# An attention and MLP kernel on one core: a written order for the first head pairs, and float64 weights decoded with an integer addition

## The chip, the cores and the metric

The kernel runs on one core of a Trainium2 chip. The core has TensorE (PE, matrix products), VectorE (DVE), ScalarE (ACT), GpSimd (POOL) and SyncE (SP, which here issues most DMA transfers); each runs its own queue in order, and semaphores tie them together. SBUF is the memory on the chip with 128 partitions (rows), PSUM holds PE's results in banks. The metric is the device time of one execution in microseconds (us); a smaller time is better.

## The reference

Float32 attention with a local band and a few global keys, four batches of eight heads over 768 positions of 64 values, is followed by a gated MLP whose weights come as float64:

```python
scores = scale * np.matmul(q, k.transpose(0, 1, 3, 2))
keep = (pos[None, :] < n_global) | ((rel >= 0) & (rel < n_local))      # 8 and 96
scores = np.where(keep, scores - slopes * dist, -1e9)
a = exp(scores - max);  a = a / (sum(a) + 1e-9);  x = a @ v            # x: 3072 x 512
h = x @ w_in                                                           # 512 -> 2048
g = h * np.clip(h + 3.0, 0.0, 6.0) / 6.0
out = (g @ w_out).astype(np.float32)                                   # 2048 -> 512
```

## The kernel before

**Work.** The 3072 tokens are eight blocks of 384. A block's attention goes by head pairs (four a block), a pair by three tiles of 128 queries. A tile's scores are 128 x 232 for each of two heads (96 earlier positions, 8 global ones, 128 of its own; 128 x 128 for a sequence's first tile). `scores` (matmul, line 765) writes them to PSUM; DVE adds a scaled distance and takes the row's minimum (L776, `n<-sp` or `n<-acc`); ACT takes exponentials and row sums (L780); `sum_up` (L788, L789, DVE) and `normalize` (L798 on POOL, L796 on DVE for the very first pair) scale the rows; `turn` has PE transpose them (L806, L808) and ACT evict them as `pt` (L810); `values` (L850) multiplies with v, and ACT and DVE split the result into a high and a low part, `xh` and `xl` (L150, L151).

**MLP.** The hidden width is cut into 16 parts f. For a block and an f, `first` does 12 matmuls (L164, `hp`), the gate makes `g`, `gh`, `gl` (L175 on ACT, L176 on DVE, L184 on ACT or L182 on POOL, L189 on DVE), and `second` does 9 matmuls (L196). One block and one f together, 21 matmuls, are called a PE block below.

**Weights.** They lie in HBM as float64, in 32 chunks of 128 x 512 (two 32-bit words each), one of `w_in` and one of `w_out` for every f. `fetch` loads chunk i into one of two buffers `wst`; the decoding makes a float32 of each and splits it into a high and a low part for PE. Per chunk: ACT takes the magnitude of the high word (L362) and later the high part (L406); DVE does seven operations (L381 clamp, L394 shift, L400 sign, L409 exponent, L384 low word times exponent, L398 float addition, L391 low part). `decode` is a generator that is advanced in four steps a chunk; `work(pe, dve)` adds up what PE and DVE are given in the written program and advances it whenever DVE has been given less than PE. `LEAD` is put on DVE's account at the start, so it sets how late the decoding begins.

**Start.** `banded_setup` blanks the halves of the q columns that must be zero (DVE memsets, L281), loads the first pairs' keys and q (`load`, L295: three transfers a pair for the first twelve pairs), and `banded_masks` makes the distances d0 and d1 on DVE from the two bounds, which come by a DMA on ACT's queue. `distances` scales them for each head (L323 on ACT for the first, L325 on POOL for the others). The first twelve pairs have unsplit operands and are worked on first; from the ninth pair on, the first MLP blocks run between them.

**What sets the order.** The instructions of PE, SP and POOL keep the order of the written program (`in_order`). ACT's and DVE's order is set by a scheduler, which simulates the program and may put an instruction ahead of one that is written before it.

Of the kernel before, what the change touches and what calls it, by code (L numbers as in the profile page):

```python
# [9 lines left out]
F32 = mybir.dt.float32  # L10
# [9 lines left out]
P = 128  # L20
# [14 lines left out]
VW = 2 * NT * P  # L35
LOAD = KW + QW + VW
# [10 lines left out]
LEAD = 5.0  # L47
# [9 lines left out]
class Kernel:  # L57
# [189 lines left out]
    def banded_masks(self, pool):  # L247
# [18 lines left out]
        ts(out=glo, in0=glo, scalar1=ng, scalar2=FAR, op0=ALU.is_ge, op1=ALU.mult)  # L266
        for d, cols in ((d0, slice(CB, W)), (d1, slice(0, W))):
            ts(out=far[:, cols], in0=rel[:, cols], scalar1=nl, scalar2=FAR, op0=ALU.is_ge, op1=ALU.mult)
            tt(out=d, in0=rel[:, cols], in1=far[:, cols], op=ALU.max)
            if d is d0:  # L270
                ts(out=glo, in0=glo, scalar1=nl, scalar2=None, op0=ALU.max)
                tt(out=d[:, 0:NG], in0=d[:, 0:NG], in1=glo, op=ALU.min)
            else:
                nc.vector.tensor_copy(out=d[:, PREV:CB], in_=glo)

    def rooms(self, pool, n, start=0):

        room = [pool.tile([P, LOAD], F32, name=f"load{start + i}") for i in range(n)]
        for i, at in enumerate(room):
            for j in range(2):  # L280
                self.nc.vector.memset(at[(1 - j) * D:(2 - j) * D, KW + j * TB:KW + (j + 1) * TB], 0.0)  # L281
        return room
# [21 lines left out]
    def loaded(self, n):  # L304
# [3 lines left out]
        q = at[:, KW:KW + QW].rearrange("p (j t c) -> p j t c", j=2, t=NT)  # L308
        v = at[:, KW + QW:LOAD].rearrange("p (s t c) -> p s t c", s=2, t=NT)
        return at[:, 0:KW], q, v[:, 0], v[:, 1]  # L310
# [28 lines left out]
    def banded_setup(self):  # L339
# [4 lines left out]
        self.room = self.rooms(self.const, ROOMS)  # L344
        self.iv = self.const.tile([P, 4], I32, name="iv")
# [582 lines left out]
```

## Time and profile before

| | us |
|---|---|
| median of 3 runs | 675.11 (674.5 to 675.69) |
| the profiled execution | 674.97 |
| its span, first to last instruction | 673.1 |
| PE busy in the span | 655.3 (97%) |
| DVE busy | 438.3 (65%) |
| ACT busy | 283.0 (42%) |
| POOL busy | 192.9 (29%) |

The profile is of one execution. Its span leaves out 1.87 us before the first and behind the last instruction. A busy PE is one with a matmul in it, at whatever pace; idle time of an engine costs only where another waits for it.

### The profile page before, as it was taken

The numbers are of one execution on the slowest core, as the hardware profiler recorded it, in microseconds if no ns is written. First come the engines' busy times: TensorE is split into PE (matmuls) and PEld (weight loads), VectorE is DVE, ScalarE is ACT, GpSimd is POOL, SyncE is SP. The second block draws the span as 40 slices with busy tenths as digits, with TensorE's granted clock in tenths as the row PEclk, the third lists the DMA queues.
The fourth block names the chain that finished last, engine by engine and source line by source line (L and its number), as shares of the span: only waits on it lengthen the run. The fifth ranks groups of instructions, "written<-read, shape, count | busy, mean of one in ns | idle before, by whom it ended". The sixth has DMA issues, their size and how long they took to land.

```text
span 673.1 us, 11323 instructions
## 1 busy us (share of the span) xinstructions
PE 655.3 (97%) x3905; PEld 588.5 (87%) x3905; DVE 438.3 (65%) x1186; ACT 283.0 (42%) x744; POOL 192.9 (29%) x354
## 2 busy tenths in 40 slices
PE   5999999999999999999999999999999999999996
PEld 4788889999999889899989999899989999989995
DVE  7789999999975666457653676447762666422221
ACT  6998755544446333144333433143331443131111
POOL 2765500000000443234340343315431343302110
PEclk9999999999999999999999999999999999999999
DMA  8677533333303456624654367534555255510001
GB/s 259 164 226 242 162 121 102 118 108 112 95 31 133 131 135 181 157 94 131 167 139 119 101 172 193 144 94 126 139 159 140 80 151 141 139 48 1 1 1 52
DMA packets 62611, 84.33 MB, mean 125 GB/s; under 512 B 8784, under 2 KB 48720, under 8 KB 62544
## 3 DMA queue, kind: packets, MB, share of 16 engines
q1 hardware_dynamic: 62256, 83.25, 43.1%
q8 instruction: 33, 0.54, 0.3%
q14 instruction: 34, 0.28, 0.1%
q10 hardware_dynamic: 288, 0.26, 0.1%
HBM read 62.52 MB, written 20.97 MB: 124 GB/s over the span
## 4 chain that ended last, share of the span: by engine, by line
PE 87%; DMA 4%; ACT 4%; DVE 2%; POOL 2%; issue 1%; SPq 0%; POOLq 0%; ACTq 0%
PE hp L164 38%; PE acc L196 32%; DMA wst<-w 4%; PE xp L850 2%; PE sp L769 2%; PE tp L850 2%; PE sp L196 2%; PE tp L196 2%; PE xp L196 2%; PE tp L769 2%; ACT n L780 2%; POOL n L798 1%; PE acc L765 1%; ACT pt L810 1%; PE acc L850 1%
## 5 line engine op out<-in xcount | busy, mean ns | idle before, releaser
L175 ACT ACTIVATE g<-hp,small 128x384 f32<-128x384 f32 x127 | 73.9, 582 | 256.2 <-PE hp L164 221.2
L164 PE MATMUL hp<-xh,w1h 128*128 128x384 f32 x512 | 174.0, 340 | 0.0
L164 PE MATMUL hp<-xh,w1l 128*128 128x384 f32 x512 | 172.8, 337 | 0.0
L164 PE MATMUL hp<-xl,w1h 128*128 128x384 f32 x512 | 171.9, 336 | 0.0
L182 POOL TENSOR_SCALAR gh<-g 128x384 fp32r<-128x384 f32 x96 | 57.8, 602 | 294.8 <-DVE g L176 264.9
L196 PE MATMUL acc<-w2h,gl 128*128 128x512 f32 x336 | 132.9, 395 | 0.1
L196 PE MATMUL acc<-w2l,gh 128*128 128x512 f32 x336 | 132.8, 395 | 0.0
L196 PE MATMUL acc<-w2h,gh 128*128 128x512 f32 x336 | 132.1, 393 | 0.0
L798 POOL TENSOR_SCALAR n<-n,sums 128x232 f32<-128x232 f32 (+1 forms) x186 | 105.0, 581 | 52.3 <-DVE sums L789 38.7
L176 DVE SCALAR_TENSOR_TENSOR g<-g,hp 128x384 f32<-128x384 f32 x128 | 70.2, 548 | 76.4 <-ACT g L175 75.9
L780 ACT ACTIVATE n<-n,least 128x232 f32<-128x232 f32 (+1 forms) x192 | 89.5, 468 | 39.2 <-DVE least L776 38.5
L189 DVE TENSOR_TENSOR gl<-g,gh 128x384 fp32r<-128x384 f32 x128 | 73.1, 571 | 45.7 <-POOL gh L182 44.1
L164 PEld LDWEIGHTS hp<-xh,w1h 128*128 128x128 f32 x512 | 96.3, 188 | 5.5 <-issue 1.5
L164 PEld LDWEIGHTS hp<-xl,w1h 128*128 128x128 f32 x512 | 96.2, 188 | 3.8
L164 PEld LDWEIGHTS hp<-xh,w1l 128*128 128x128 f32 x512 | 96.0, 188 | 0.0
L196 PEld LDWEIGHTS acc<-w2l,gh 128*128 128x128 f32 x336 | 63.0, 188 | 13.3
L196 PEld LDWEIGHTS acc<-w2h,gl 128*128 128x128 f32 x336 | 63.2, 188 | 11.8 <-DVE gl L189 1.5
L196 PEld LDWEIGHTS acc<-w2h,gh 128*128 128x128 f32 x336 | 63.3, 188 | 10.6 <-POOL gh L182 0.3
L823 DVE STREAM_TRANSPOSE blocks<-n 128x256 f32<-128x256 f32 x112 | 43.5, 424 | 25.7 <-POOL n L798 25.1
L743 POOL TENSOR_SCALAR kx<-load 64x504 fp32r<-64x504 f32 (+1 forms) x40 | 23.1, 577 | 119.2 <-PE hp L164 117.6
L776 DVE CUSTOM_DVE_ANT_0 n<-sp,d 128x232 f32<-128x232 f32 (+1 forms) x70 | 23.7, 376 | 37.1 <-PE sp L769 36.8
L780 ACT ACTIVATION_READ_ACCUMULATOR n<-n,least 128x1 f32 x192 | 36.5, 190 | 0.0
(111 smaller groups left out, 764.9 us busy)
## 6 DMA issues: line engine op xcount, KB each, us to landing
wst<-w SPq DMA_DIRECT2D x32, 512.0 KB, 3.5
there<-blocks SPq DMA_DIRECT2D x52, 256.0 KB, 2.6
load<-pairs SPq DMA_DIRECT2D x20, 636.0 KB, 5.3
load<-pairs SPq DMA_DIRECT2D x32, 384.0 KB, 4.1
weights<-there SPq DMA_DIRECT2D x48, 192.0 KB, 3.8
out<-o SPq DMA_DIRECT2D x23, 256.0 KB, 2.1
weights<-there SPq DMA_DIRECT2D x32, 160.0 KB, 3.3
load<-pairs SPq DMA_DIRECT2D x12, 252.0 KB, 4.5
```

What stands on the lines that cost most here:

```text
L164: self.nc.tensor.matmul(hp, lhsT=self.w1(w, f)[:, kt, :], rhs=a[:, kt, :], start=(n == 0), stop=(n == 3 * NKT - 1))
L175: nc.scalar.activation(out=g, in_=hp, func=AF.Relu, bias=self.three, scale=1.0)
L176: nc.vector.scalar_tensor_tensor(out=g, in0=g, scalar=6.0, in1=hp, op0=ALU.min, op1=ALU.mult)
L182: self.nc.gpsimd.tensor_scalar(out=gh, in0=g, scalar1=1.0, scalar2=0.0, op0=ALU.mult, op1=ALU.add)
L189: self.nc.vector.tensor_tensor(out=gl, in0=g, in1=gh.bitcast(F32), op=ALU.subtract)
L196: self.nc.tensor.matmul(acc[tt], lhsT=a[:, tk], rhs=self.w2(w, f), start=(f == 0 and j == 0), stop=(f == NF - 1 and j == 2))
L769: nc.tensor.matmul(sp[:, j, lo:W], lhsT=q[:, t], rhs=part["kx"][:, c], start=(m == 0), stop=(m == 1))
L776: nc.vector.tensor_tensor_reduce(out=e[:, j, lo:W], in0=sp[:, j, lo:W], in1=d, op0=ALU.add, op1=ALU.min, scale=scale, scalar=3.0e38, accum ...
L780: nc.scalar.activation(out=e[:, j, lo:W], in_=e[:, j, lo:W], func=AF.Exp, bias=self.least[:, i:i + 1], scale=-1.0, accum_out=self.sums[:, ...
L798: nc.gpsimd.tensor_scalar(out=e[:, j, lo:W], in0=e[:, j, lo:W], scalar1=over, scalar2=0.0, op0=ALU.mult, op1=ALU.add)
L823: nc.vector.transpose(out=blocks[:, :, s].rearrange("p b j q -> p j b q"), in_=e[:, :, c:c + P].rearrange("p j (b q) -> p j b q", b=4))
L850: nc.tensor.matmul(xps[j * D:(j + 1) * D, t * P:(t + 1) * P], lhsT=vt[0:K, t, j * D:(j + 1) * D], rhs=self.part(t, j, c, K), start=(c == 0 ...
```

## The change

Five things are edited. The columns of a load are laid out anew, so that the first twelve pairs need two transfers of 64 rows instead of three, and the second of the very first goes on ACT's queue; the blanks are one range a half, written by DVE for the first room, by POOL for the other two. The masks are made with fewer operations on DVE and the small ones on POOL. Four matmuls on constants are put ahead of everything on PE (`wake`). ACT and DVE keep the written order, too, until the loop reaches pair number `HEAD` = 1, and `LEAD` goes from 5 to 13. The decoding takes the low word on POOL, as a multiple of the last place, and DVE adds it to the bits as integers; the exponent (L409) and the product (L384) go, and a chunk is fetched one chunk earlier.

```diff
-LEAD = 5.0
+HEAD = 1
+LEAD = 13.0
+WAKE = 4
...
-        ts(out=glo, in0=glo, scalar1=ng, scalar2=FAR, op0=ALU.is_ge, op1=ALU.mult)
-        for d, cols in ((d0, slice(CB, W)), (d1, slice(0, W))):
-            ts(out=far[:, cols], in0=rel[:, cols], scalar1=nl, scalar2=FAR, op0=ALU.is_ge, op1=ALU.mult)
-            tt(out=d, in0=rel[:, cols], in1=far[:, cols], op=ALU.max)
...
+        pool_ts(out=glo, in0=glo, scalar1=ng, scalar2=FAR, op0=ALU.is_ge, op1=ALU.mult)
+        pool_ts(out=glo, in0=glo, scalar1=nl, scalar2=0.0, op0=ALU.max, op1=ALU.add)
+        ts(out=far, in0=rel, scalar1=nl, scalar2=FAR, op0=ALU.is_ge, op1=ALU.mult)
+        tt(out=d0, in0=rel[:, CB:W], in1=far[:, CB:W], op=ALU.max)
+        tt(out=d0[:, 0:NG], in0=d0[:, 0:NG], in1=glo, op=ALU.min)
+        tt(out=d1[:, 0:PREV], in0=rel[:, 0:PREV], in1=far[:, 0:PREV], op=ALU.max)
+        tt(out=d1[:, CB:W], in0=rel[:, CB:W], in1=far[:, CB:W], op=ALU.max)
+        nc.gpsimd.tensor_copy(out=d1[:, PREV:CB], in_=glo)
...
+    def blank(self, room, engine):
+
+        engine.memset(room[D:P, KQ:KW + QW], 0.0)
+        engine.memset(room[0:D, 0:TB], 0.0)
...
-                parts = [(slice(0, KW), slice(None))] + [(slice(KW + j * TB, KW + (j + 1) * TB), slice(j * D, (j + 1) * D)) for j in range(2)]
+                parts = [(slice(TB, KW + QW), slice(0, D)), (slice(0, KQ), slice(D, P))]
             for columns, rows in parts:
-                self.nc.sync.dma_start(out=self.place(n)[rows, columns], in_=self.pairs[n, rows, columns])
+                engine = self.nc.scalar if n == 0 and rows == slice(D, P) else self.nc.sync
+                engine.dma_start(out=self.place(n)[rows, columns], in_=self.pairs[n, rows, columns])
...
+    def wake(self):
+
+        any_ = self.three.broadcast_to([P, P])
+        out = self.ps_x.tile([P, BANK], F32, name="xp")[:, 0:P]
+        for _ in range(WAKE):
+            self.nc.tensor.matmul(out, lhsT=any_, rhs=any_, start=True, stop=True)
...
     def magnitude(self, i):
+        words = self.raw[i].rearrange("p (c w) -> p c w", w=2)
         self.z[i] = self.zp.tile([P, DM], I32, name="wz")
...
+        self.e[i] = self.ep.tile([P, DM], I32, name="we")
+        self.nc.scalar.activation(out=self.z[i].bitcast(F32), in_=words[:, :, 1].bitcast(F32), func=AF.Abs)
+        self.nc.gpsimd.tensor_scalar(out=self.e[i], in0=words[:, :, 0].bitcast(U32), scalar1=2.0 ** -29, scalar2=0.0, op0=ALU.mult, op1=ALU.add)
...
-                stt(out=e, in0=words(i - 1)[:, :, 0].bitcast(U32), scalar=2.0 ** -52, in1=e, op0=ALU.mult, op1=ALU.mult)
-                if i + 1 < N:
-                    self.fetch(i + 1)
...
-                tt(out=e, in0=self.z.pop(i - 1).bitcast(F32), in1=e, op=ALU.add)
...
-                ts(out=self.e[i], in0=z, scalar1=-0x00800000, scalar2=None, op0=ALU.bitwise_and)
...
+                if i + 2 < N:
+                    self.fetch(i + 2)
+            yield 0.6 * a
+            if a:
+                tt(out=z, in0=z, in1=self.e.pop(i), op=ALU.add)
...
+            yield 0.69 * a
...
-        self.in_order(start)
+        self.in_order(start, here(), (mybir.EngineType.PE, mybir.EngineType.SP, mybir.EngineType.Pool))
+        self.in_order(begin, head, (mybir.EngineType.Activation, mybir.EngineType.DVE), True)
```

The program's order shows it at three places. SP first, at the start: `load` is a room for a pair's keys, q (first transfers) and values (128x768), `wst` a weight chunk, and a number behind a name tells the rooms apart. Before:

```order
L295 DMA load_72<-pairs 128x504
L295 DMA load_72<-pairs 64x384 x2
L295 DMA load_73<-pairs 128x504
L295 DMA load_73<-pairs 64x384 x2
L357 DMA wst<-w 128x1024
L295 DMA load_164<-pairs 128x504
L295 DMA load_164<-pairs 64x384 x2
L357 DMA wst<-w 128x1024
L295 DMA load_72<-pairs 128x768
L295 DMA load_73<-pairs 128x768
L295 DMA load_72<-pairs 128x504
```

And of the change:

```order
L300 DMA load_72<-pairs 64x888
L300 DMA load_73<-pairs 64x888 x2
L300 DMA load_165<-pairs 64x888 x2
L300 DMA load_72<-pairs 128x768
L371 DMA wst<-w 128x1024
L300 DMA load_73<-pairs 128x768
L371 DMA wst<-w 128x1024
L300 DMA load_72<-pairs 64x888 x2
```

The first chunk has moved behind the third pair's keys and the first pair's values, and the fourth pair's keys (`load_72` again) follow the second chunk with one transfer fewer.

ACT next, from its first scaled distance `p` to the third pair's exponentials (`n,sums<-n,least`, two a tile); `wz<-wst` is a chunk's magnitude. Before:

```order
L323 ACTIVATE p_177<-d_91 128x128 x2
L780 ACTIVATE n,sums<-n,least 128x128 x2
L323 ACTIVATE p_178<-d_92 128x232
L780 ACTIVATE n,sums<-n,least 128x232
L362 ACTIVATE wz<-wst 128x512
L780 ACTIVATE n,sums<-n,least 128x232 x3
L780 ACTIVATE n,sums<-n,least 128x128 x2
L780 ACTIVATE n,sums<-n,least 128x232 x2
L362 ACTIVATE wz<-wst 128x512
L810 COPY pt<-tp 128x2x128
```

And of the change:

```order
L328 ACTIVATE p_179<-d_87 128x128 x2
L328 ACTIVATE p_180<-d_88 128x232
L797 ACTIVATE n,sums<-n,least 128x128 x2
L797 ACTIVATE n,sums<-n,least 128x232 x4
L797 ACTIVATE n,sums<-n,least 128x128 x2
L797 ACTIVATE n,sums<-n,least 128x232 x4
L797 ACTIVATE n,sums<-n,least 128x128 x2
L827 COPY pt<-tp 128x2x128
```

The second distance stands ahead of the first exponentials, and no magnitude stands between the exponentials of the first three pairs; the two magnitudes come six rows later.

DVE last, in the decoding while two token blocks share the weights. `g` and `gl` are the gate, `ISA` is the new addition. Before:

```order
L176 SCALAR_TENSOR_TENSOR g<-g,hp 128x384
L381 TENSOR_SCALAR wz<-wz 128x512
L384 SCALAR_TENSOR_TENSOR we<-wst,we 128x512
L394 TENSOR_SCALAR wz<-wz 128x512
L189 TENSOR_TENSOR gl<-g,gh 128x384
L398 TENSOR_TENSOR we<-wz,we 128x512
L400 SCALAR_TENSOR_TENSOR wz<-wst,wz 128x512
L176 SCALAR_TENSOR_TENSOR g<-g,hp 128x384
L409 TENSOR_SCALAR we<-wz 128x512
L391 TENSOR_TENSOR w2l_1350<-we,w2h_1349 128x512
```

And of the change:

```order
L179 SCALAR_TENSOR_TENSOR g<-g,hp 128x384
L413 ISA wz<-wz,we 128x1024
L398 TENSOR_SCALAR wz<-wz 128x512
L192 TENSOR_TENSOR gl<-g,gh 128x384
L399 TENSOR_SCALAR wz<-wz 128x512
L404 TENSOR_TENSOR w1l_1336<-wz,w1h_1335 128x4x128
L407 SCALAR_TENSOR_TENSOR wz<-wst,wz 128x512
L179 SCALAR_TENSOR_TENSOR g<-g,hp 128x384
```

A whole chunk now lies between two gates, in five operations; before, five of a chunk's seven lay between two gates.

## Rows read from the trace of the kernel before

**Rows 1.** Busy time by stretch: stretch, length, engines' busy us, clock, DMA share, GB/s.

```profile
0.00:5.16 5.16, 0.94 (x3) 0.77 (x4) 3.44 (x14) 1.49 (x3) 1.41 (x10) 1.00 0.51 154
5.16:22.17 17.01, 13.08 (x79) 10.49 (x80) 13.92 (x71) 12.79 (x47) 7.72 (x17) 1.00 0.81 245
22.17:57.17 35.00, 33.47 (x287) 28.68 (x286) 30.89 (x130) 33.65 (x113) 21.74 (x42) 1.00 0.77 222
57.17:95.00 37.83, 36.63 (x272) 32.30 (x273) 35.83 (x90) 26.69 (x70) 14.82 (x22) 1.00 0.54 171
95.00:205.00 110.00, 110.00 (x551) 99.43 (x550) 100.11 (x202) 54.29 (x97) 1.22 (x2) 1.00 0.28 91
205.00:673.00 468.00, 461.22 (x2720) 416.84 (x2718) 254.10 (x686) 154.13 (x418) 145.95 (x263) 1.00 0.43 118
```

**Rows 2.** PE's waits in the first 22 us: total, times, longest.

```profile
PE sp L765 <- DMA load<-pairs: 4.2, 1, 4.2
```

**Rows 3.** PE's waits from 22 to 95 us.

```profile
PE tp L806 <- POOL n L798: 1.4, 4, 0.6
PE tp L806 <- ACT pt L810: 1.2, 3, 0.5
```

**Rows 4.** The chain that ended last: start, length in us, what.

```profile
4.22 5.97 DMA wst<-w
...
95.07 2.08 PE acc L196 x9
97.16 2.10 PE hp L164 x12
```

**Rows 5.** Timeline of ACT: start, length, what, idle time before it.

```profile
10.21 0.67 ACT L362 ACTIVATE wz<-wst 128x512 f32<-128x512 f32 x1 [1.78 <-DMA wst<-w]
```

**Rows 6.** Timeline of DVE in the first 8 us.

```profile
1.00 2.89 DVE L281 MEMSET load<- 64x384 f32 x6
3.89 0.17 DVE L263 CAST fv<-iv 128x4 f32<-128x4 int32 x1
...
7.41 0.40 DVE L776 CUSTOM_DVE_ANT_0 n<-acc,p 128x232 f32<-128x232 f32 x1
```

**Rows 7.** DMA issues of the first 8 us: KB each, us to landing.

```profile
load<-pairs SPq DMA_DIRECT2D x3, 252.0 KB, 3.3
load<-pairs SPq DMA_DIRECT2D x6, 96.0 KB, 3.5
iv<-bounds ACTq DMA_DIRECT2D x1, 2.0 KB, 3.1
```

**Rows 8.** Timeline of PE in the first 22 us.

```profile
5.48 3.06 PE L765 MATMUL acc<-load 128*128 128x232 f32 x8
...
8.82 1.73 PE L765 MATMUL acc<-load 128*128 128x232 f32 x8
...
20.73 1.32 PE L850 MATMUL xp<-pt,load 128*64 128x128 f32 x20
```

**Rows 9.** Groups of DVE from 95 to 205 us: busy us, mean ns, idle.

```profile
L176 DVE SCALAR_TENSOR_TENSOR g<-g,hp 128x384 f32<-128x384 f32 x27 | 14.9, 550 | 6.4 <-ACT g L175 6.3
L384 DVE SCALAR_TENSOR_TENSOR we<-wst,we 128x512 f32<-128x512 uint32 x21 | 14.3, 683 | 0.0
L398 DVE TENSOR_TENSOR we<-wz,we 128x512 f32<-128x512 f32 x21 | 14.3, 683 | 0.0
```

**Rows 10.** Timeline of DVE around 101 us.

```profile
101.33 0.68 DVE L398 TENSOR_TENSOR we<-wz,we 128x512 f32<-128x512 f32 x1
101.93 0.42 DVE L394 TENSOR_SCALAR wz<-wz 128x512 int32<-128x512 int32 x1
```

**Rows 11.** The page's costliest groups, one of POOL.

```profile
L182 POOL TENSOR_SCALAR gh<-g 128x384 fp32r<-128x384 f32 x96 | 57.8, 602 | 294.8 <-DVE g L176 264.9
```

**Rows 12.** Groups of DVE from 60 to 95 us.

```profile
L398 DVE TENSOR_TENSOR we<-wz,we 128x512 f32<-128x512 f32 x6 | 4.4, 736 | 0.0
```

**Rows 13.** Groups of POOL from 60 to 95 us.

```profile
L798 POOL TENSOR_SCALAR n<-n,sums 128x232 f32<-128x232 f32 x12 | 9.6, 815 | 0.0
```

More of the change, by code (lines that the diff above doesn't have):

```diff
@@ L458, in banded @@
     def banded(self, flag):
+        here = lambda: len(self.nc.cur_bb.bb.instructions)
+        begin = here()
         self.banded_setup()
-        start = len(self.nc.cur_bb.bb.instructions)
+        start = here()
         self.common(2, 2)
@@ L486, in banded @@
                 self.room += self.rooms(self.pool("more", 1, ctx=ctx), MORE - ROOMS, ROOMS)
+                self.blank(self.room[2], self.nc.gpsimd)
                 self.load(2, False)
+                self.load(0, True)
+                self.fetch(0)
+                self.load(1, True)
                 self.fetch(1)
[L489 to L490 removed]
                 self.plain_distances(ctx)
@@ L563, in banded, with in_order @@
         self.finish()
-        self.in_order(start)
+        self.in_order(start, here(), (mybir.EngineType.PE, mybir.EngineType.SP, mybir.EngineType.Pool))
+        self.in_order(begin, head, (mybir.EngineType.Activation, mybir.EngineType.DVE), True)
         return acc
-    def in_order(self, start):
+    def in_order(self, start, end, engines, first=False):
         last = {}
-        for i in self.nc.cur_bb.bb.instructions[start:]:
-            if i.engine in (mybir.EngineType.PE, mybir.EngineType.SP, mybir.EngineType.Pool) and "Tile" not in type(i).__name__:
+        for n, i in enumerate(self.nc.cur_bb.bb.instructions[start:None if first else end], start):
+            if i.engine in engines and "Tile" not in type(i).__name__:
                 if i.engine in last:
@@ L574, in in_order @@
                         mybir.DependencyClass.NoSync, mybir.DependencyReason.DATA), reason="in_order")
-                last[i.engine] = i.name
+                if n < end:
+                    last[i.engine] = i.name
     def attention(self, i, x, first):
@@ L741, in split @@
                 part["kx"] = kk.hp.tile([P, KW], F32R, name="kx")
-                nc.scalar.mul(out=part["q1"], in_=q[:, j], mul=scale)
+                nc.scalar.mul(out=part["q1"], in_=q[j], mul=scale)
                 nc.gpsimd.tensor_scalar(out=part["kx"][own, c], in0=k[own, c], scalar1=1.0, scalar2=0.0,
@@ L745, in split @@
             elif step == 1:
-                nc.vector.scalar_tensor_tensor(out=part["q2"], in0=q[:, j], scalar=scale, in1=part["q1"].bitcast(F32),
+                nc.vector.scalar_tensor_tensor(out=part["q2"], in0=q[j], scalar=scale, in1=part["q1"].bitcast(F32),
                                                op0=ALU.mult, op1=ALU.subtract)
@@ L764, in scores @@
             if self.plain:
-                nc.tensor.matmul(sp[:, j, lo:W], lhsT=queries[:, j, t], rhs=keys[:, c], start=True, stop=True)
+                nc.tensor.matmul(sp[:, j, lo:W], lhsT=queries[j][:, t], rhs=keys[:, c], start=True, stop=True)
             else:
```

74 lines of the change are left out of this document (28 added, 46 removed).

## The prediction

> **What bounds the kernel now.** I read the busy times by stretch first [rows 1]. From 95 to 205 us TensorE (PE) is busy 110.00 of 110.00 us, and after 205 us it idles 6.8 of 468; the change leaves the order of every engine behind the last weight alone, so nothing can come from there. PE's idle time that the change can reach is 5.16 - 0.94 and 17.01 - 13.08 us in the first two stretches, and 1.53 + 1.20 from 22.17 to 95. Of it 4.2 us are the wait for the first load [rows 2]; behind 22 us transposes wait, 1.4 us for rows that GpSimd (POOL) normalizes and 1.2 us for evictions by ScalarE (ACT) [rows 3].
>
> The chain of waits says what the head hangs on [rows 4]: the landing of the first weight chunk, 5.97 us. ACT's queue holds that chunk's magnitudes ahead of most of the first exponentials; ACT stands 1.78 us for the chunk, and everything behind it in the queue stands too [rows 5]. The head (up to the fourth head pair) is so bound by ACT's queue and not by PE: from 5.16 us, ACT's first scaled distance, to 22.17, its first exponential of the fourth pair, ACT is busy 12.79 of 17.01 us [rows 1]. After that both are nearly full (ACT 33.65 and PE 33.47 of 35.00).
>
> **The change, part by part.** Masks, blanks and loads. VectorE (DVE) loses four of its six blanking memsets and starts no sooner for it: they end at 3.89, and the bounds land 3.1 us after their issue at 0.73, so its cast starts at about 3.89 either way [rows 6, 7]. What follows is shorter: 232 columns are compared once instead of 128 and then 232, and the tiny operations go to POOL, which is idle there. Today DVE reads the second tile's scores at 7.41 [rows 6], held by the second distance scale, which ACT does only behind the first exponentials. In the new order both scales stand ahead of them, so I put that read at about 6.1. PE's first matmul still needs loads that land around 4.2; the second queue for half of a load saves one issue, and the three transfers of an early pair become two. Nothing is counted for either, since PE's start is not what DVE waits for. The issue on ACT's queue delays ACT's table load, which is hidden: ACT has nothing to do before 5.16.
>
> The four waking matmuls cost nothing: PE idles until 4.22. Today the first eight matmuls of 232 columns take 3.06 us and the next eight 1.73 [rows 8], although the granted clock of the stretch reads 1.00, that is 2.4 GHz [rows 1]; the first ran nearer half of it, after an engine idle since the start. The waking may give these 1.3 us back. The sum takes 0, because the slow matmuls run to 8.5 us, while DVE has still to read the second tile.
>
> ACT's head. Its work to the fourth pair is today's 12.79 us less one weight cast, some 0.6 like the other passes over a chunk [rows 5]; two magnitudes stay there, but behind the exponentials, when the chunks have long landed. Its idle time is 4.22. DVE's decoding leaves the head too (today 13.92 busy of 17.01), so DVE can follow. I keep 0.9 of idle for normalizing that DVE now does between the scores: 5.1 + 12.2 + 0.9 = 18.2 against 22.17, a gain of 4.0. The upper bound is 4.9, with no idle left. The lower one comes from the fourth pair's keys: three pairs of keys before them, 1.33 MB, values 0.77, two chunks 1.02, and their own 0.45 MB; 154 GB/s brings 0.79 MB by 5.16, and the other 2.78 at today's 245 GB/s land at 16.5 [rows 1]. About 1.4 us of matmuls later the first values could begin, at 17.9 instead of 20.73 [rows 8]: a gain of 2.8.
>
> From there to 95 us. The later decoding takes three operations of about 0.65 us out of ACT between the fourth pair and the first gate (by the order, 3 casts stand ahead of it instead of 5), and each chunk is fetched a whole chunk ahead, so waits for chunks shrink. PE can win its idle time there, 2.73 us, and little more. I take 2.4; bounds 0 and 3.5 (a wait also costs the refilling of PE's pipe).
>
> Decoding. Of seven DVE operations a chunk two go, one of 0.683 and one of 0.42 us [rows 9, 10]. POOL gains one of 128x512. The trace has no such operation; the nearest row of its kind is 602 ns for 128x384 [rows 11], so 0.8 us by columns, bounds 0.6 and 1.2. From 95 to 205 us POOL is busy 1.22 us and hides it; from 57 to 95 it is busy 14.82 of 37.83 [rows 1]. The new addition prints as an instruction of 128x1024 where the others have 512. Bounds: 0.68, an addition today, and 1.2, the same per column for twice the columns. I take 0.77, since the kernel's own budget gives it 0.69 where it gives 0.60 to those of 0.68.
>
> DVE in that stage, for one PE block of 4.18 us (12 + 9 matmuls, 2.10 + 2.08 [rows 4]): by the order 21 chunks stand between the fifth gate and the twenty-second, 1.235 a block (0.875 today). A DVE operation hides 0.08 of itself behind the next: one of 0.68 starts at 101.33, the next at 101.93 [rows 10]. So a chunk costs 2 x 0.34 + 2 x 0.60 + 0.69 = 2.57 (today 3 x 0.34 + 4 x 0.60 = 3.42), and the two gate operations of 0.55 [rows 9] cost 0.94: together 0.94 + 1.235 x 2.57 = 4.11, plus POOL's disturbance. Where POOL works beside decoding, the DVE addition takes 736 ns against 683 [rows 9, 12], the largest rise there; if all seven kinds rose so, six chunks beside 18 POOL operations lose 7 x 6 x 0.053 / 18 = 0.12 us a POOL operation. I take half, 0.06, and come to 4.18: DVE is full to the brim. A gate has slack, since its four operations of about 0.55 need 2.2 of the 4.18 us until PE uses their product; so 2.0 us of lateness are free. I book -0.2. What is freed in all, 0.85 x 32 = 27 us of DVE, is worth nothing by itself: PE does not wait there.
>
> Sum: 4.0 + 2.4 - 0.2 = 6.2. The profiled execution took 674.97 us for its span of 673.1, so 668.8; it lies 0.14 below the median of 675.11, which changes nothing.
>
> **The rivals.** Two times of this kernel that differ by under 0.2%, 1.35 us, can hardly be told apart.
>
> (a) The put-off decoding comes due. By the order four chunks stand ahead of DVE's first gate instead of six, and chunk 0 cannot be added before POOL has passed the sixth pair's normalizing. If PE reaches its first block (57.17 today) before the weights, one chunk's DVE work, 2.57 us, is paid back: 671.4; with both late chunks 673.9. For it: only 12% of DVE is free from 22 to 57 us (30.89 of 35.00), and POOL now waits in its queue for chunks, with the normalizing of pairs behind, for which PE's transposes wait. Against it: a block's second product comes 10 us after its first, and a chunk is less work.
>
> (b) The addition takes 1.2 us, 0.43 more. Over those 17 blocks 17 x 1.235 x 0.43 - 2.0 of slack = 7.0 us are lost: 674.97 - 6.4 + 7.0 = 675.6. It cancels the gain from 1.17 us on.
>
> (c) Slower: DVE stands for the whole of each POOL operation, 0.62 us (0.8 less what its own running operation covers) instead of 0.06. 17 x 1.235 x 0.56 - 2.0 = 9.8, so 674.97 - 6.4 + 9.8 = 678.4; from 0.40 us extra on no gain is left. Against it stand the 736 ns: where both work, POOL is stretched, 0.815 us for 232 columns [rows 13], and DVE hardly. The Trainium skill (SBUF — State Buffer, "Who interferes with whom") has (c) as its rule: whichever of the two starts first holds the shared port pair for its whole instruction. The trace bears it out on POOL's side alone.
>
> (d) No gain: the keys come too slowly, since all early loads of keys are now transfers of 64 rows. At 197 GB/s the 2.78 MB take 14.1 us, the fourth pair's land at 19.3, the head's 4.0 are gone, and one chunk of (a) takes the rest: 675.3. For it: today's transfers of 64 rows, 96 KB, take 3.5 us in the first 8 us, and those of 252 KB over 128 rows 3.3 [rows 7]. Against it: only half of those bytes have this form, and transfers of 128 rows run beside them. The Trainium skill (SBUF — State Buffer, "Door 1: The DMA port swizzle") gives 196 GB/s for 64 rows against 328 for 128, and little for issuing both halves at once. By it alone (d) would be the forecast.
>
> **How the numbers follow.** The forecast, 665 to 670.5 us, 0.60; better, with PE's pipe and ACT quite full, 0.05; (a) with one chunk or (d) in part, 670.5 to 673.5, 0.17; (a) with both and (d), 0.09; (b) 0.03; (c) 0.06. Faster: 0.60 + 0.05 + 0.17, and 0.01 of the mixed cases, 0.83; same 0.11; slower 0.06. The range from 664.5 to 673.0 leaves out half of the better cases, a little of the third and the last three: 0.2.
>
> **What would show it.** Right: ACT's first exponential of the fourth pair near 18.2, the first value matmul near 16.5, PE's first block near 51, hardly a wait of PE for ACT behind it, the last weight ready some seven blocks (30 us) sooner, and from there the same 468 us; the first scores at the faster pace. Wrong: the fourth pair near 20 (loads), PE waiting at its first `hp`, an `ISA` row of over 1 us, DVE rows stretched beside POOL's `we`, and PE idle between 95 and 170.

## The result: slower, and the profile after

The change takes 678.78 us (median of 5 runs, 678.25 to 679.37) against 675.11 for the kernel before: a ratio of 1.0049 on record, 95% interval 1.0036 to 1.0061 (the quotient of the two medians is 1.0054). The forecast was 668.8, with 664.5 to 673.0 as its range. The profiled execution has a span of 677.0 us. Its stretches, in the form of [rows 1] (stretch, length, busy us of PE, PE's weight load, DVE, ACT and POOL, granted clock, DMA share, GB/s):

```profile
0.00:5.16 5.16, 2.08 (x8) 1.78 (x8) 2.04 (x8) 1.49 (x2) 3.98 (x17) 1.00 0.54 125
5.16:22.17 17.01, 15.80 (x91) 13.77 (x92) 11.52 (x70) 13.22 (x50) 7.92 (x22) 1.00 0.96 261
22.17:57.17 35.00, 34.15 (x292) 29.82 (x291) 25.20 (x113) 31.96 (x109) 21.49 (x45) 1.00 0.75 216
57.17:95.00 37.83, 34.48 (x253) 30.56 (x253) 34.75 (x83) 27.81 (x72) 19.58 (x26) 0.95 0.52 173
95.00:205.00 110.00, 108.16 (x535) 95.99 (x534) 84.26 (x156) 52.86 (x94) 17.81 (x22) 1.00 0.29 92
205.00:677.00 472.00, 465.25 (x2740) 420.18 (x2738) 257.20 (x692) 155.49 (x421) 145.79 (x264) 1.00 0.42 117
```

The head is better filled, as forecast. But from 57 to 95 us PE is busy for 34.48 instead of 36.63 us, and from 95 to 205 it idles 1.84 us, where it had no idle time at all before. What PE waited for, from 22 to 205 us (total, times, longest; before, [rows 3]):

```profile
PE sp L782 <- DVE least L793: 1.9, 1, 1.9
PE tp L823 <- ACT pt L827: 1.5, 1, 1.5
PE sp L199 <- ACT gh L187: 1.1, 1, 1.1
PE tp L823 <- POOL n L815: 0.8, 1, 0.8
PE sp L199 <- DVE gl L192: 0.4, 1, 0.4
```

PE's order is fixed by the program, so the same matmul can be looked up in both traces and its two start times subtracted. This is the most useful reading of this case, for it says where time is won and lost. Four places serve below: the first values (20.73 us before), PE's first block (its first `hp`, 57.17), the seventh block (96.99) and the thirty-third (206.17, when all weights have been decoded). Each start is that of one profiled execution.

| | first values | block 1 | block 7 | block 33 |
|---|---|---|---|---|
| the change against before, us | -1.83 | -3.06 | +0.51 | +4.00 |

So 3.06 us are won up to the first block, 3.57 lost from there to the seventh, 3.49 lost from the seventh to the thirty-third, and nothing happens behind. Of the 3.49, 1.75 are lost up to the ninth block (+2.26) and 1.74 in small steps behind it.

**The head.** PE's first scores start at 5.72 us instead of 4.22. The chain of waits begins with a load (start, length, what), and further on a chunk's load stands in it, which lands at 55.24:

```profile
1.15 4.45 DMA load<-pairs
...
48.28 6.96 DMA wst<-w
```

The first is the half of a load that went on ACT's queue. The DMA issues of the first 8 us (KB each, median us from issue to landing, the time behind earlier transfers included; [rows 7] before):

```profile
load<-pairs SPq DMA_DIRECT2D x5, 222.0 KB, 5.5
...
load<-pairs ACTq DMA_DIRECT2D x1, 222.0 KB, 4.4
```

The numbers are larger than before, but five transfers stand behind each other here, so they do not show that the form of 64 rows is slower; in E8 below, with the keys over 128 rows, the first scores start at 5.59. DVE waits for these scores (in brackets the idle time just before), and reads the second tile's at 8.61, where it was 7.41 before:

```profile
7.07 0.29 DVE L793 CUSTOM_DVE_ANT_0 n<-sp,p 128x128 f32<-128x128 f32 x1 [1.52 <-PE sp L782]
...
8.61 0.40 DVE L793 CUSTOM_DVE_ANT_0 n<-acc,p 128x232 f32<-128x232 f32 x1 [1.03 <-PE acc L782]
```

ACT's first exponential of the fourth pair:

```profile
21.40 0.42 ACT L797 ACTIVATE n<-n,least 128x128 f32<-128x128 f32 x1
```

**The second loss: DVE stands beside POOL.** DVE's costliest groups from 95 to 205 us (busy us, mean ns, idle time), and POOL's new operation there:

```profile
L413 DVE CUSTOM_DVE_ANT_0 wz<-wz,we 128x1024 uint16<-128x1024 uint16 x21 | 16.8, 799 | 0.4
L192 DVE TENSOR_TENSOR gl<-g,gh 128x384 fp32r<-128x384 f32 x25 | 15.1, 606 | 4.1 <-ACT gh L187 4.1
...
L179 DVE SCALAR_TENSOR_TENSOR g<-g,hp 128x384 f32<-128x384 f32 x26 | 14.3, 548 | 20.4 <-ACT g L178 20.4
L398 DVE TENSOR_SCALAR wz<-wz 128x512 f32<-128x512 f32 x20 | 10.0, 498 | 0.7 <-ACT wz L379 0.6
...
L380 POOL TENSOR_SCALAR we<-wst 128x512 int32<-128x512 uint32 x20 | 16.9, 843 | 56.6 <-DMA wst<-w 53.3 <-DVE wz L407 3.3
```

The addition reads 799 ns, the gate's `gl` 606 and the clamp 498, but `g` 548 as before [rows 9]. The timeline shows what a mean hides. In this pair of rows `gl` starts 0.08 us after POOL's operation, and takes 1.00 us instead of 0.55; it ends 0.41 us after POOL's:

```profile
117.35 0.67 POOL L380 TENSOR_SCALAR we<-wst 128x512 int32<-128x512 uint32 x1 [2.73 <-DMA wst<-w]
117.43 1.00 DVE L192 TENSOR_TENSOR gl<-g,gh 128x384 fp32r<-128x384 f32 x1
```

In the next pair POOL starts while DVE is at the sign (L407), and POOL is the one that is stretched; `g`, which reads one operand from PSUM, starts beside POOL and keeps its 0.55:

```profile
124.35 0.69 DVE L407 SCALAR_TENSOR_TENSOR wz<-wst,wz 128x512 int32<-128x512 int32 x1
124.67 0.89 POOL L380 TENSOR_SCALAR we<-wst 128x512 int32<-128x512 uint32 x1 [2.66 <-DMA wst<-w]
124.95 0.55 DVE L179 SCALAR_TENSOR_TENSOR g<-g,hp 128x384 f32<-128x384 f32 x1
```

Sorted by which engine started first, the rows of 95 to 205 us fall apart (mean ns, number of rows in brackets; worked out from the start times in the trace):

| DVE's operation | no POOL operation beside it | DVE started first | POOL started first |
|---|---|---|---|
| addition (L413) | 681 (4) | 685 (6) | 905 (11) |
| `gl` (L192) | 551 (19) | 545 (2) | 895 (4) |
| clamp (L398) | 414 (14) | none | 695 (6) |
| `g` (L179) | 549 (20) | 554 (2) | 543 (4) |

So the whole lengthening lies in 21 operations that started behind POOL, about one for each of POOL's. The sign, the shift and the low parts never did so here, and keep their times.

**Both losses: ACT stands for a chunk.** From the timelines of ACT and PE; in brackets the idle time just before, and what ended it:

```profile
55.32 0.67 ACT L379 ACTIVATE wz<-wst 128x512 f32<-128x512 f32 x1 [1.41 <-DMA wst<-w]
56.77 0.58 ACT L827 COPY pt<-hp 128x512 f32<-128x512 f32 x1
...
99.77 0.67 ACT L379 ACTIVATE wz<-wst 128x512 f32<-128x512 f32 x1 [1.52 <-DMA wst<-w]
100.34 0.50 ACT L187 CAST gh<-g 128x384 fp32r<-128x384 f32 x1
...
58.71 0.30 PE L823 MATMUL tp<-ident,n 128*128 128x128 f32 x1 [1.45 <-ACT pt L827]
100.89 0.51 PE L199 MATMUL sp<-w2h,gh 128*128 128x512 f32 x1 [1.12 <-ACT gh L187]
```

ACT waits at a magnitude for its chunk to land; an eviction (56.77) and a gate's cast (100.34) wait behind it in the queue, and PE waits for them. From 95 to 170 us ACT stands 16.4 us in this way; before it was 11.1.

**The clock.** PE waits once for 1.89 us (DVE had stood for a magnitude and then beside POOL), and the matmuls behind the wait run slower, 0.52 us each instead of 0.34, until 75.84. From 65 to 80 us the granted clock is 0.89 on the average, before it was 1.00: 2.4 GHz, and for a part of the stretch the lower level of 1.2. This cost PE about 1.4 us: the third block begins level with before, and the fourth 1.42 late.

```profile
71.45 1.05 PE L782 MATMUL sp<-load 128*128 128x232 f32 x4 [1.89 <-DVE least L793]
...
73.28 0.52 PE L167 MATMUL hp<-xl,w1h 128*128 128x384 f32 x1
...
76.09 0.34 PE L167 MATMUL hp<-xl,w1h 128*128 128x384 f32 x1
```

The stretch that holds them, in the columns of the first table:

```profile
65.00:80.00 15.00, 13.11 (x87) 11.44 (x87) 12.51 (x35) 10.19 (x29) 6.28 (x10) 0.89 0.52 187
```

### The profile page after: what moved, and what is told of

It reads as the page before. It is cut to its first block, busy times and chain, and to the rows that moved or that the text cites. A ratio compares the mean times of both kernels' runs of the same rounds, so it can differ in the third digit from the quotient of the medians.

```text
span 677.0 us, 11398 instructions
## 1 busy us (share of the span) xinstructions
PE 659.9 (97%) x3913; PEld 592.1 (87%) x3913; DVE 415.0 (61%) x1115; ACT 282.8 (42%) x744; POOL 216.6 (32%) x393
## 4 chain that ended last, share of the span: by engine, by line
PE 75%; DVE 10%; DMA 5%; issue 3%; ACT 3%; POOL 2%; POOLq 0%; SPq 0%; ACTq 0%; DVEq 0%
PE hp L167 34%; PE acc L199 31%; DMA wst<-w 4%; PE xp L867 2%; PE sp L786 2%; POOL n L815 2%; DVE wz L407 2%; PE tp L867 2%; PE tp L786 2%; DVE wz L413 1%; DVE n L793 1%; DVE gl L192 1%; ACT n L797 1%; DVE wz L398 1%; DVE wz L399 1%
## 5 line engine op out<-in xcount | busy, mean ns | idle before, releaser
L179 DVE SCALAR_TENSOR_TENSOR g<-g,hp 128x384 f32<-128x384 f32 x128 | 70.2, 548 | 91.5 <-ACT g L178 91.2
L815 POOL TENSOR_SCALAR n<-n,sums 128x232 f32<-128x232 f32 (+1 forms) x186 | 100.7, 558 | 42.4 <-DVE sums L806 28.8
L192 DVE TENSOR_TENSOR gl<-g,gh 128x384 fp32r<-128x384 f32 x128 | 75.4, 589 | 49.2 <-POOL gh L185 44.0
L380 POOL TENSOR_SCALAR we<-wst 128x512 int32<-128x512 uint32 x32 | 26.0, 812 | 74.3 <-DMA wst<-w 68.3
L793 DVE CUSTOM_DVE_ANT_0 n<-sp,d 128x232 f32<-128x232 f32 (+1 forms) x70 | 23.7, 376 | 37.0 <-PE sp L786 36.7
L797 ACT ACTIVATION_READ_ACCUMULATOR n<-n,least 128x1 f32 x192 | 37.3, 194 | 0.0
```

Of the source, the lines that this page charges most:

```text
L179: nc.vector.scalar_tensor_tensor(out=g, in0=g, scalar=6.0, in1=hp, op0=ALU.min, op1=ALU.mult)
L192: self.nc.vector.tensor_tensor(out=gl, in0=g, in1=gh.bitcast(F32), op=ALU.subtract)
L793: nc.vector.tensor_tensor_reduce(out=e[:, j, lo:W], in0=sp[:, j, lo:W], in1=d, op0=ALU.add, op1=ALU.min, scale=scale, scalar=3.0e38, accum ...
L797: nc.scalar.activation(out=e[:, j, lo:W], in_=e[:, j, lo:W], func=AF.Exp, bias=self.least[:, i:i + 1], scale=-1.0, accum_out=self.sums[:, ...
L815: nc.gpsimd.tensor_scalar(out=e[:, j, lo:W], in0=e[:, j, lo:W], scalar1=over, scalar2=0.0, op0=ALU.mult, op1=ALU.add)
```

## The experiments

Unless a diff says otherwise, each is the changed kernel with one edit, compared with runs of the kernel before on the same chip. All have a new program, and where its operations or buffers differ, the scheduler orders ACT and DVE behind the head somewhat anew. The theories, as the expectations name them: C, contention of DVE with POOL; Q, ACT's queue stands for chunks; A, the decoding that was put off comes due. Where an expectation speaks of 5.8 us of lengthening, it adds up what each operation took over the lower quartile of its kind between 95 and 170 us. The last four columns give the start of a matmul minus that of the same matmul before, in the one profiled execution; it took 679.72 us in E4, the shortest of six, and lay 1.0 to 3.0 us above the median in E5, E10, E11 and E18. The ratios are those on record, and not quotients of the medians.

| run | median us | ratio (95%) | first values | block 1 | block 7 | block 33 |
|---|---|---|---|---|---|---|
| E1 no low words | 675.05 | 0.9992 (0.9981-1.0003) | -1.79 | -2.33 | -1.61 | -0.18 |
| E2 POOL in quarters | 677.79 | 1.0037 (1.0027-1.0047) | -1.67 | -2.82 | -0.05 | +2.65 |
| E3 POOL twice | 689.03 | 1.0208 (1.0190-1.0226) | -2.38 | -3.38 | +0.91 | +13.26 |
| E4 low words on DVE | 683.02 | 1.0117 (1.0099-1.0135) | -1.55 | +0.84 | +3.98 | +4.03 |
| E5 new head, old decoding | 688.06 | 1.0180 (1.0164-1.0196) | -2.04 | +2.03 | +12.10 | +13.50 |
| E6 old head, new decoding | 677.83 | 1.0032 (1.0021-1.0044) | -2.01 | -0.88 | -0.16 | +2.08 |
| E7 three buffers | 674.92 | 0.9992 (0.9983-1.0001) | -1.06 | -3.32 | -1.55 | -0.80 |
| E8 keys over 128 rows | 675.76 | 1.0004 (0.9988-1.0019) | -1.16 | -3.69 | -2.37 | +0.70 |
| E9 LEAD 5 | 680.61 | 1.0081 (1.0068-1.0095) | -2.17 | +0.30 | +1.64 | +4.37 |
| E10 E7 and E8 | 676.75 | 1.0016 (1.0004-1.0028) | +2.07 | +0.47 | +0.63 | +2.95 |
| E11 E10, low words on ACT | 680.61 | 1.0071 (1.0053-1.0089) | +2.60 | +2.44 | +7.82 | +7.82 |
| E12 E10, LEAD 9 | 678.91 | 1.0050 (1.0032-1.0068) | +0.82 | +1.03 | +2.44 | +3.88 |
| E13 E7, third chunk later | 673.94 | 0.9971 (0.9960-0.9982) | -1.87 | -4.10 | -2.13 | -1.41 |
| E14 E13 and E8 | 674.12 | 0.9975 (0.9965-0.9984) | -1.81 | -4.05 | -2.12 | -1.40 |
| E15 E13, no low words | 674.19 | 0.9976 (0.9965-0.9987) | -1.54 | -2.00 | -1.15 | -1.14 |
| E16 E14, in quarters | 675.78 | 1.0007 (0.9995-1.0018) | -1.56 | -3.38 | -2.47 | -0.12 |
| E17 E14, SP's queue alone | 676.49 | 1.0003 (0.9989-1.0018) | +0.92 | -1.35 | +0.39 | +1.13 |
| E18 before, three buffers | 683.45 | 1.0114 (1.0092-1.0136) | +0.44 | +3.19 | +6.46 | +10.28 |

In E4, E5, E8, E10, E11, E12, E17 and E18 the time fell in none of the ranges that the expectation gave; E2 fell between two, and E9 and E16 ended 0.6 and 0.7 us beyond one.

**E1, E2, E3: less, cut and more of POOL's work.**

```diff
-        self.nc.gpsimd.tensor_scalar(out=self.e[i], in0=words[:, :, 0].bitcast(U32), scalar1=2.0 ** -29, scalar2=0.0, op0=ALU.mult, op1=ALU.add)
```

E1 has a tile of zeros for `self.e[i]` in its place, E2 the same line four times on a quarter of the columns each, E3 the line twice.

> Leaves out GpSimd's rounding of the low words: the addition takes a tile of zeros, so the last bits of the weights are missing. Theory C (contention): after 57 us a VectorE operation that starts while GpSimd works on a chunk's low words stands until GpSimd is done; between 95 and 170 us this lengthens VectorE's operations by 5.8 us and costs TensorE 3.5. Without them that stretch loses under 1 us and the run takes 674 to 676. Theory Q (queue): ScalarE stands in its queue at the magnitude for the next chunk (16.4 us between 95 and 170), and the gate's cast behind it is late; nothing of that is changed here, so 678 to 679.5.

> GpSimd's operation of 128x512 in four of 128x128. Theory C, if VectorE stands for the GpSimd instruction in progress: at most a quarter of the wait at each, VectorE's lengthening between 95 and 170 falls from 5.8 to 1.5 to 3 us, and the run takes 676 to 677.5. If VectorE stands for all of GpSimd's work, however cut: 678.5 to 680. Theory Q: as the change, 678 to 679.5.

> GpSimd does each chunk's low words twice. Theory C: another 0.2 to 0.6 us of VectorE for each of some 28 chunks after 57 us, VectorE has no room for it between 95 and 170, so 683 to 690. Theory Q: GpSimd has room, 678 to 680.

C was right in E1 and E3. Without the work the run is 3.7 us faster than the change, with twice the work 10.3 us slower, and 12.35 of E3's us are lost between blocks 7 and 33 (some 1.5 of them may be the lower clock there, 0.98 on the average from 95 to 170 us). In E1 DVE's groups of 95 to 205 us read nearly as before:

```profile
L179 DVE SCALAR_TENSOR_TENSOR g<-g,hp 128x384 f32<-128x384 f32 x27 | 14.9, 552 | 23.8 <-ACT g L178 23.4
L192 DVE TENSOR_TENSOR gl<-g,gh 128x384 fp32r<-128x384 f32 x26 | 14.4, 553 | 4.1 <-ACT gh L187 4.1
L415 DVE CUSTOM_DVE_ANT_0 wz<-wz,zero 128x1024 uint16<-128x1024 uint16 x20 | 13.7, 685 | 0.1
...
L400 DVE TENSOR_SCALAR wz<-wz 128x512 f32<-128x512 f32 x19 | 8.0, 420 | 1.6 <-ACT wz L382 1.6
```

Against these rows the change's addition is 114 ns longer, `gl` 53 and the clamp 78: 21 x 0.114 + 25 x 0.053 + 20 x 0.078 = 5.3 us for 20 POOL operations, 0.26 us each. Between blocks 1 and 7 E1 loses 0.72 us instead of 3.57, and its clock does not fall there. Yet it still loses 1.43 us between blocks 7 and 33, which C does not explain.

Quarters (E2) help by 1.0 us, and not by the hoped-for three quarters. A quarter is no quarter of the time: 472 ns each, 37.3 us in all where the whole ones took 16.9. POOL is in DVE's way more often, for a shorter while.

```profile
L381 POOL TENSOR_SCALAR we<-wst 128x128 int32<-128x128 uint32 x79 | 37.3, 472 | 33.8 <-DMA wst<-w 20.5 <-DVE wz L408 9.5
```

**E4: the low words on DVE.** POOL's line goes; ahead of the fetch stands, and the account is raised to 1.2:

```diff
+                ts(out=self.e[i], in0=self.raw[i].rearrange("p (c w) -> p c w", w=2)[:, :, 0].bitcast(U32), scalar1=2.0 ** -29, scalar2=0.0, op0=ALU.mult, op1=ALU.add)
```

> VectorE rounds the low words itself, a sixth operation of some 0.6 us a chunk, and the kernel's account of its work is raised by 0.6; GpSimd does nothing in the decoding. Theory C: no operation is lengthened between 95 and 170; a chunk costs VectorE 3.2 us instead of 3.42 in the kernel before, so that stretch loses nothing, and the head's 3 us are kept in part: 672 to 675. Theory Q: ScalarE waits for chunks as in the change, 677 to 680.

It missed: 683.02. Behind the seventh block C is right in the profiled execution, and nothing is lost there (+3.98 to +4.03), with six DVE operations a chunk. But the head is lost, 3.0 us of waits for POOL's normalizing among it: with the sixth operation the scheduler puts decoding between the pairs' scores and sums, and POOL gets its rows late. DVE itself, which now reads a chunk first, stands 4.2 us for one at 52.31.

**E5 and E6: each half of the change alone.** E5 has the functions of the old decoding in the changed kernel, E6 the new ones in the kernel before.

> The new head, loads and LEAD of 13 with the decoding of before (seven VectorE operations a chunk, nothing on GpSimd). If the loss behind 57 us comes from the new decoding (theory C and its queues): the head's 3 us are kept, 671.5 to 673.5. If it comes from the decoding that was put off (theory A: the first block's weights are late because the decoding begins later): TensorE still loses 2 to 4 us between 55 and 80 us, and a chunk costs more VectorE time than in the change, 674.5 to 678.

> The head, loads and LEAD of before with the new decoding alone. Theory C: VectorE is full between 95 and 170 us and lengthened by 5 to 6 us there, and nothing is gained ahead of it: 677.5 to 681. Theory A: the decoding is not put off here, so TensorE loses nothing that it doesn't lose before: 674 to 676.

E6's time is in C's range, though DVE is not full there: busy 66.17 of the 75 us from 95 to 170. E5 went further than A: with the old, longer decoding and LEAD at 13 PE waits for weights and for rows, and 10 us are lost between blocks 1 and 7. Its waits from 22 to 105 us begin:

```profile
PE tp L829 <- POOL n L821: 3.7, 3, 2.6
PE hp L167 <- ACT w1h L420: 3.7, 3, 1.6
PE hp L167 <- DVE w1l L405: 1.8, 2, 1.4
```

The halves do not add up: 12.4 and 2.2 us apart, 3.7 together. The new head can only be afforded with the shorter decoding. It is not the only source of the early gain, either: E6, with the old one, has its first values 2.01 us sooner, 1.0 of it because its first chunk landed sooner than in the profile of before, with the same loads (the magnitude starts at 9.20 instead of 10.21). Leads in the head carry such scatter.

**E7, E13, E15: a third buffer for chunks.** E7 fetches the third chunk behind the second. E13 puts that one load behind the fourth pair's keys. E15 is E13 with E1's zeros.

```diff
-            self.decoding(words, 2, 2, side="right")
+            self.decoding(words, 3, 2, side="right")
...
-                if i + 2 < N:
-                    self.fetch(i + 2)
+                if i + 3 < N:
+                    self.fetch(i + 3)
...
                 self.fetch(1)
+  E7:          self.fetch(2)
...
                                     self.load(2, True)
+  E13:                             self.fetch(2)
```

> A third buffer for a chunk's words, each chunk fetched one chunk sooner. Theory Q: ScalarE's 16.4 us of waiting for chunks between 95 and 170 and the 6.3 between 55 and 95 nearly vanish, and TensorE's losses of 3.6 us between 55 and 95 with them, perhaps half of those behind: 673.5 to 676. Theory C: VectorE stays full and lengthened, 677.5 to 680.

> The third buffer, its first chunk loaded behind the fourth pair's keys. Head as in the change again, first values near 18.9 (19.68 with the load ahead); behind it as with the third buffer, 0.7 to 0.9 us lost between 95 and 170: 673.7 to 674.7. If the buffer's gain hangs on chunk 2 coming early: 675.5 to 677.

> The same as e13 without GpSimd's low words (a tile of zeros is added). If lengthening and chunk waits add up: what is left of e13's loss between 95 and 205 goes, and some of 57 to 95: 671.5 to 673.2. If either alone gives VectorE all the room that it needs: the same as e13 within 0.6.

E7 came out in Q's range, 2.6 us below C's. ACT's waits for chunks are gone: the first rows of its waits from 95 to 170 us in E13 name none.

```profile
ACT g L178 <- PE hp L167: 11.4, 10, 2.5
ACT gh L187 <- DVE g L179: 6.0, 17, 1.2
ACT wz L379 <- DVE w1l L404: 6.0, 8, 1.6
```

DVE's operations are lengthened as much as in the change (in E13 `gl` reads 671 ns and the shift 511: 27 x 0.118 + 19 x 0.089 = 4.9 us against E1's rows), and still PE loses little. Loss between blocks 7 and 33, in brackets its parts up to the ninth block and behind it:

| | chunks waited for | third buffer |
|---|---|---|
| POOL rounds low words | the change: 3.49 (1.75 + 1.74) | E13: 0.72 (0.04 + 0.68) |
| no low words | E1: 1.43 (1.07 + 0.36) | E15: 0.01 |

Each cure gives most of it back, and both give all. The two are not quite apart: without POOL's work ACT's waits for chunks also shrink, from 16.4 us to 9.5 in E1. The likely reading is that both take the same slack from two sides, so that together they cost more than the sum; that is argued and not shown. From 95 to 170 us DVE is busy 73.74 of 75 us in the change, 68.57 in E1, 70.18 in E13 and 64.61 in E15. In E13 DVE has done more decoding ahead of 95 us: 13 additions instead of 11. E15's forecast of a sum failed and its other one held: it is not faster than E13, since it starts the first block 2.1 us later.

E13 takes 673.94 and beats both kernels, 0.9971 (0.9960 to 0.9982) of the one before.

**E8 and E9: the loads, and LEAD.**

```diff
-  E8:           parts = [(slice(TB, KW + QW), slice(0, D)), (slice(0, KQ), slice(D, P))]
+  E8:           parts = [(slice(TB, KQ), slice(None)), (slice(KQ, KW + QW), slice(0, D)), (slice(0, TB), slice(D, P))]
-  E9: LEAD = 13.0
+  E9: LEAD = 5.0
```

> The first twelve pairs' keys loaded over 128 rows (and q in two transfers of 64 rows, as before the change), all else as changed. If the transfers of 64 rows hold the head up: TensorE's first scores some 1 us sooner than 5.72, the first values some 1 us sooner than 18.90, and the run 677 to 678.3. If the head's pace is ScalarE's alone: first values within 0.3 us of 18.90, 678.3 to 679.5.

> The change with LEAD at 5 as before: six chunks instead of three stand ahead of VectorE's first gate by the order. Theory A (put-off decoding comes due): TensorE's 3.6 us lost between 55 and 95 shrink to 1 or 2, and VectorE has room behind, since more chunks are done: 674 to 676.5. Theory C alone: VectorE's operations are lengthened as before and the pace of chunks is the same, so 678 to 680.

E8 is 3 us faster than the change, but not for the reason given: its first scores start at 5.59 and the first values are later by 0.7. Between blocks 1 and 7 it loses 1.3 us instead of 3.57; its clock stays at 1.00 there and its waits come to 1.5 us for ACT and 0.7 for DVE. Behind, it loses 3.1. ACT waits for chunks as long as in the change (16.5 us from 95 to 170), so it is not the total of these waits that sets the loss, but what stands behind each. The scheduler's order of DVE differs from the change's in many rows; which of them does it is not settled. In E9 the later losses shrink as A says, from 3.57 to 1.34 us and from 3.49 to 2.73, but with more chunks done early the head loses all its gain (+0.30 at block 1), and the time does not fall: the decoding costs PE earlier instead of later. LEAD at 13 instead of 5 is worth about 2 us.

**E10, E11, E12, E14, E16, E17: combinations.** E10 is E7 with E8's loads; E11 adds that ACT rounds the low words (an activation with scale 2^-29), E12 a LEAD of 9. E14 is E13 with E8's loads, E16 adds E2's quarters, and E17 issues the whole first load on SP's queue.

> The third buffer and the loads of 128 rows together. If each takes away its own loss (3.9 us the buffer, 3.0 the loads, measured one at a time): 672 to 673. If both give back the same room of VectorE between 95 and 170, of which there are 3.5 us only once: 674 to 675.5.

> As the run with both, but ScalarE rounds the low words instead of GpSimd, 32 operations of some 0.68 us. Theory C: VectorE's lengthening between 95 and 170 falls from 5.3 us to under 0.5, ScalarE has 32 us of room there, but between 22 and 57 it is busy 33 of 35 us already and takes two or three more: if the second weighs less, 671 to 673, else 674 to 677.

> As the run with both, with LEAD at 9 instead of 13. Theory A: about two chunks more stand ahead of the first gate, and TensorE's waits between 55 and 95 shrink by about 1 us more: 0.5 to 1.5 us below the run with both. If ScalarE and VectorE have no room ahead of 57 us: the pairs come later by as much, and it is the same within 0.5.

> The same with the early keys over 128 rows. If e10's lost head came from the third chunk's place in the queue: no wait for a load over 1 us before 22 us, first values between 18.6 and 19.8, 673 to 674.5. If it came from one more transfer a pair: first values over 21 again, 676 to 677.5.

> As e14 with GpSimd's operation in four. Its lengthening of VectorE between 95 and 170 was 4.55 us in quarters against 5.8: 0 to 0.5 us below e14. If quarters only put GpSimd's queue off: the same or up to 1 us above.

> As e14, with all of the first load on SyncE's queue. If the second queue holds the start up (its transfer shares the DMA engines with those behind the first half): TensorE's first scores at 4.2 to 4.6 instead of 5.6, and 672.6 to 673.6 if the head keeps it. If the start hangs on the blanks or the masks: first scores at 5.3 or later, 673.7 to 674.6.

None beats E13. E10 shows how narrow the head is: with the third chunk ahead of the fourth pair's keys and one transfer more a pair, PE waits 3.11 us for those keys, and runs slower behind (four matmuls of 232 columns in 1.75 us instead of 0.95):

```profile
12.80 0.95 PE L783 MATMUL acc<-load 128*128 128x232 f32 x4
...
18.86 1.19 PE L783 MATMUL sp<-load 128*128 128x128 f32 x4 [3.11 <-DMA load<-pairs]
...
20.27 1.75 PE L783 MATMUL acc<-load 128*128 128x232 f32 x4
```

E14 takes that wait away by the chunk's place alone, as expected. E17 has it again (2.7 us) without the chunk in front; why is not settled. Its earlier first scores (4.51 against 5.37 us in E14) are worth little: the second half of them waits for its load until 5.66, the first eight matmuls of 232 columns take 3.30 us in both, and DVE reads the first scores at 6.57 instead of 6.71. E11 bears C out once more, nothing is lost behind block 7, but 5.4 us are lost between blocks 1 and 7, where ACT has the work in its place. E12's lower LEAD costs 2.2 us instead of winning 1. E16's quarters are worse than whole ones once chunks come in time.

**E18: the kernel before with the third buffer** (the same edit, `fetch(i + 2)` where it has `fetch(i + 1)`).

> The kernel before with a third buffer for a chunk's words and each chunk fetched one sooner, nothing else. If e13's gain is the buffer's alone: 673 to 674.5. If the buffer only mends what the change lacks (TensorE loses nothing between 95 and 205 before): 674.5 to 676.

Slower by 1.1%. The third magnitude goes ahead of the fourth pair's exponentials on ACT, and 3.2 us are lost before the first block; PE waits most there for rows that POOL normalizes (3.5 us from 22 to 95), and how much of it the magnitude causes is not settled. E13's gain is the gain of the new head and decoding with the chunks' waits mended, not the buffer's own.

## Why the prediction was wrong, step by step

Each of the three terms of the sum failed, by about as much. The head brought 0.8 of its 4.0 us. The stretch from there to the seventh block was to bring 2.4 and lost 1.3 (from 0.8 ahead to 0.51 behind). The decoding lost 3.49 instead of 0.2. The shortfalls of 3.2, 3.7 and 3.3 us are the 10 us between 668.8 and 678.78.

**The decoding in the stage with two blocks**: "I take half, 0.06, and come to 4.18: DVE is full to the brim" and "I book -0.2". That DVE would be full was right. The step that failed is the size of the disturbance: 0.26 us a POOL operation and not 0.06. The addition itself was cheaper than taken (0.685 for 0.77), so a block needs 0.94 + 1.235 x (2.485 + 0.26) = 4.33 us of DVE for PE's 4.18. Over 17 blocks that is 2.6 us, 0.6 after the 2.0 of slack; E13, where POOL works and no chunk is waited for, lost 0.72. The change lost 3.49, for ACT's waits for chunks took PE's time here, too, which the sum did not have: the 1.75 us up to the ninth block, of which E1 still lost 1.07 and E13 0.04. The row that the 0.06 rested on [rows 12] was the wrong witness: where DVE runs without a gap, POOL is the one that waits, and its own rows are stretched [rows 13]. Here ACT and POOL start at the landing of a chunk, so POOL often starts ahead of DVE's next operation. Rival (c) had this mechanism, at 0.62, and a chance of 0.06; the price came out between. That its time, 678.4, lies near the measured one is chance, since it kept 6.4 us of gain ahead of this stage, and none was left there. E1 and E3 show the price. The Trainium skill (SBUF — State Buffer, "Who interferes with whom") adds what tells `g` from the others: a DVE instruction with at most one SBUF input, outside the fast two-port modes, does not contend. Here `g` with its operand in PSUM keeps 543 ns behind POOL while `gl` and the addition are lengthened; the trace agrees. The clamp has one input and is lengthened; no row here shows its mode.

**The stage from 22 to 95 us** was to bring 2.4 us, since "waits for chunks shrink". They did not: ACT waited 7.8 us for chunks from 22 to 95 us, as before, and from 95 to 170 it waited longer. A buffer is free after the sign, the load takes 3.5 us, and only then can the magnitude begin. The chunk that landed at 55.24 held an eviction up for which PE then waited. I had looked at how early a fetch is issued and not at how fast the loop around two buffers can turn. The loss of 3.57 us has the 1.45 and 1.89 us of PE's waits and 1.4 of the lower clock in it, less what was won back. E7 and E13, without waits for chunks, still lose 1.8 and 2.0 there, and E1, with them, 0.7; none of the three has the lower clock. How the loss divides among the chunks, POOL's work and the clock stays open.

**The head** was to bring 4.0 at the fourth pair's first exponential. It came at 21.40 instead of 22.17, a gain of 0.8; the gain was 1.83 at the first values and 3.06 at the first block (expected there: some 6). The step that failed is "Nothing is counted for either, since PE's start is not what DVE waits for". PE's first scores started at 5.72, 1.5 us later than before, when the half of the first load on ACT's queue had landed (1.15 + 4.45 = 5.60). DVE waited for them and read the second tile's at 8.61, where 6.1 was taken, and ACT waited for DVE: it idled 3.7 us between its first scaled distance and 21.40, where 0.9 was kept. Its busy time there, 12.5 us, is about the 12.2 of the sum. Of rival (d) little came true: PE waited 0.46 us for the fourth pair's keys, until 16.35, where (d) had them land at 19.3. Behind the exponentials the magnitudes waited for no chunk, as forecast (1.8 us before); but E6, which has them between the exponentials, reaches the fourth pair's at 19.69, so that this order was what the head hung on is not shown.

**The waking matmuls** gave nothing: the first eight of 232 columns took 3.30 us (3.06 before), with the first four of 128 ahead of them 1.20. They ran while PE had nothing else to do; no run leaves them out. Between the last waking matmul and the first scores lie 2.74 us of idle PE.

**Right** were that the addition costs no more than its neighbours (685 ns undisturbed; 0.77 was taken and 1.2 in rival b), POOL's operation at 0.67 undisturbed (0.8 was taken), the lack of any effect behind the last weight, and that the weights are ready sooner: the last low part ends at 172.18, before at 195.86. These are 23.7 us of the 30 expected.

## What to carry to other kernels

An operation moved to an idle engine is priced by what it does to its neighbours: look up whether its partner can be made to wait for it, and take the row where the partner starts second. Before a delay is booked at nothing because nobody waits for it, follow its result to the engine that does: here from PE over DVE to ACT. Where an engine is to be filled to the brim, count the loop around its buffers too (landing, work, release, next landing), for there each small delay comes through. And subtracting the starts of the same matmul in two traces finds the place of a loss faster than any sum of waits.

## What the hardware showed that was not expected

Beside a busy DVE a POOL operation of 128x512 took 0.84 us on the average and one of 128x128 0.47 (E2), so four small pieces took more than twice the time of the whole. A DVE operation that started ahead of POOL's kept its time, one that started behind it took 0.22 to 0.34 us longer on the average, and `g`, with an operand in PSUM, kept its time either way. A wait of PE of 1.9 us (the change) or 3.1 us (E10) was followed by 3.3 and some 5 us of matmuls at a lower pace, while the change's wait of 1.45 us was not.
